# Attention features in (d, h) order, token-major q and k by DMA transposes, second layer norm normalised on ScalarE

## The chip, the cores and the metric

The kernel runs on one core of one Trainium2 chip. The metric is the device time of one execution in microseconds (us). Runs are compared by the median of several executions, and one further execution is profiled.

The engines of the core are named as in the profile: PE (TensorE, matrix multiply), DVE (VectorE), ACT (ScalarE), POOL (GpSimd) and SP (SyncE, which here only issues DMAs). Each works through its own instruction queue in order, and waits on semaphores for the others. DMAs are issued from SP, POOL and ACT.

## What is computed

One transformer block on 2048 tokens of 512 features in bfloat16, forward and backward. The kernel returns the output and the gradients of seven inputs.

```python
def A(x, wqkv, wo):                      # 32 heads of 16 features
    q, k, v = split(x @ wqkv)            # (2048, 1536) -> 3 x (32, 2048, 16)
    idx = pos[:, None] - 2 * arange(8)   # window of 8, dilation 2
    logits = einsum("hsd,hswd->hsw", q, k[:, idx]) / 4   # -1e9 where idx < 0
    o = einsum("hsw,hswd->hsd", softmax(logits), v[:, idx])
    return o.transpose(...).reshape(2048, 512) @ wo

def B(x, w1, b1, w2, b2):                # 512 -> 1792 -> 512
    return gelu(x @ w1 + b1) @ w2 + b2

h  = x + A(layernorm(x), wqkv, wo)
h2 = h + B(layernorm(h), w1, b1, w2, b2)
# outputs: h2 and the gradients of x, wqkv, wo, w1, b1, w2, b2 for a given grad_out
```

## The kernel before

**Three phases.** Tokens come in NC = 4 chunks of CH = 512. Phase 1 (lines 326 to 525) is the first layer norm and the attention, with the second layer norm at its end. Phase 2 (lines 570 to 643) is the feed-forward block, forward and backward; its first piece, `p2_h(0)`, is interleaved with the end of phase 1 (lines 712 to 717). Phase 3 (lines 882 to 1196) is the attention's backward pass and the weight gradients. The last two phases keep what they need of phase 1 in DRAM.

**Two layouts of q, k and v.** The projection `p1_proj` (line 341) makes q, k and v feature-major: a tile `qt`, `kt` or `vt` has 128 features on its partitions, 4 groups g of them, and 512 tokens along its rows. The features come in the order of the weight's columns, (h, d): head first, then the 16 features of a head. So one group of 128 partitions holds 8 whole heads.

The products with the window (`dots`, line 233) are made in this layout. DVE multiplies q with eight shifted views of k (line 236), and PE adds up the 16 features of each head with a 0/1 matrix `Emat[:, g]` (line 240), which puts the 8 heads of group g into 8 of 32 rows.

The weighted sums (`band`, line 257) need token-major rows instead. POOL gathers them with an indirect DMA (`gather_rows`, line 225) from DRAM tiles `v_d`, `k_d`, `q_d` and `go_d`, whose rows hold the features in the order (d, h). DVE multiplies them with the coefficients (line 266), and PE adds up with the 0/1 matrix `S32` (line 271). Phase 1 reads `v_d` only; `k_d`, `q_d` and `go_d` are read in phase 3 (line 1010).

**`to_tm_store` (line 208)** makes the token-major rows. For half a chunk, 8 PE transposes of 128x128 (line 214) go to a PSUM tile `ptm`; ACT copies it to `tmst` (line 217); SP stores it (line 219), with a copy of the border rows into the neighbour's tile (lines 221 and 223). The transposes multiply by a permutation `Pmat` and write with a stride, which turns (h, d) into (d, h). It runs for v in `p1_v`, for k and q in `p1_tm`, and for the gradient `got` in phases 2 and 3.

**Order of phase 1.** The program order is that of `p1_round(c)` (line 487): layer norm of chunk c+2, window products of c+1, output projection and second layer norm of c-1 (`p1_d`), q and k of c+2 (`p1_qk`), softmax of c+1, weighted sums of c in two halves (`p1_o`) around v of c+1 (`p1_v`), and last `p1_tm(c+1)`. The framework's scheduler then orders each engine's queue by its own estimates of when work is ready, so the order on an engine differs from that of the program. Tiles that share a tag share buffers, and the framework adds the waits.

**`layernorm` (line 169).** DVE makes the statistics of each 128-token tile (lines 173 and 174), POOL raises the variance to the power -1/2 (line 178), DVE makes `nm`, minus mean times that (line 180), and DVE normalises the four tiles (line 182). PE then transposes the result (`to_fm`, line 166) and ACT copies the transposes out (line 167). It runs for `xt` in `p1_ln` and for `h` in `p1_d`.

**Start.** `p1_ln(0)` loads the first rows of x and then the three parts of `wqkv` straight into the tile that the projection reads (line 333).

Of the kernel before, what the change touches and what calls it, by code (L numbers as in the profile page):

```python
# [10 lines left out]
P = 128  # L11
# [5 lines left out]
H = 32  # L17
# [19 lines left out]
def kernel(  # L37
# [70 lines left out]
    make_identity(nc, ident[:])  # L108
    Pmat = const.tile([P, P], BF16, name="Pmat")
    S32 = const.tile([P, 32], BF16, name="S32")  # L110
    Sum4 = const.tile([P, P], BF16, name="Sum4")
    nSum4 = const.tile([P, P], BF16, name="nSum4")
    Sm = const.tile([P, 4, P], BF16, name="Sm")
    ind8 = const.tile([P, 8], BF16, name="ind8")
    Emat = const.tile([P, 4, 32], BF16, name="Emat")
    mk = const.tile([16, 2, 4, 32], BF16, name="mk")
# [18 lines left out]
    v_d, k_d, q_d, go_d = ([dram.tile([RB, D], BF16, name=f"{n}_d{c}") for c in range(NC)] for n in ("v", "k", "q", "go"))  # L135
    vf_d = dram.tile([P, 4, SP], BF16, name="vf_d")
    ln1_d = dram.tile([S, D], BF16, name="ln1_d")
    ln2_d = dram.tile([S, D], BF16, name="ln2_d")
# [29 lines left out]

    def layernorm(wp, src, rstd_all, c, dst):
        mv = wp.tile([P, TPC, 2], F32, name="mv", tag="mv", bufs=2)  # L170
        for j in range(TPC):
            st = wp.tile([P, 6], F32, name="st6", tag="st6", bufs=2)
            V.bn_stats(out=st[:], in_=src[:, j, :])
            V.bn_aggr(out=mv[:, j, :], in_=st[:])
        rs = rstd_all[:, c * TPC:(c + 1) * TPC]
        ve = wp.tile([P, TPC], F32, name="ve", tag="ve", bufs=2)
        V.tensor_scalar(out=ve[:], in0=mv[:, :, 1], scalar1=EPS, scalar2=None, op0=ALU.add)
        G.tensor_tensor(out=rs, in0=ve[:], in1=mhalf[:], op=ALU.pow)
        nm = wp.tile([P, TPC], F32, name="nm", tag="nm", bufs=2)
        V.scalar_tensor_tensor(out=nm[:], in0=mv[:, :, 0], scalar=-1.0, in1=rs, op0=ALU.mult, op1=ALU.mult)  # L180
        for j in range(TPC):
            V.tensor_scalar(out=dst[:, j, :], in0=src[:, j, :], scalar1=rs[:, j:j + 1], scalar2=nm[:, j:j + 1],
                            op0=ALU.mult, op1=ALU.add)

# [22 lines left out]

    def to_tm_store(wp, fm, off, dst, c, back, nb=3, stage=None):
        for j2 in range(TPC // 2):
            pt = TT("ptm")  # L210
            for jj in range(2):
                j = 2 * j2 + jj
                for g in range(4):
                    T.transpose(_sub(pt[:], [[32, DH], [1, 8]], jj * 512 + 8 * g),  # L214
                                fm[:, g, off + j * P:off + (j + 1) * P], Pmat[:])
            st = stage() if stage else wp.tile([P, 2, 512], BF16, name="tmst", tag="tmst", bufs=nb)
            A.copy(out=st[:], in_=pt[:].rearrange("p (a n) -> p a n", a=2))  # L217
            r = j2 * 2 * P + (RPAD if back else 0)
            SY.dma_start(out=dst[c][r:r + 2 * P, :].rearrange("(a p) d -> p a d", p=P), in_=st[:])
            if back and j2 == 1 and c + 1 < NC:  # L220
                SY.dma_start(out=dst[c + 1][0:RPAD, :], in_=st[P - RPAD:P, 1, :])
            if not back and j2 == 0 and c > 0:
                SY.dma_start(out=dst[c - 1][CH:CH + RPAD, :], in_=st[0:RPAD, 0, :])

    def gather_rows(R, dst, c, sc, back):
# [7 lines left out]
    def dots(wp, ql, kw_, L, mask):  # L233
        for g in range(4):
            pr = wp.tile([P, W, 512], BF16, name="pr", tag="prod", bufs=2 + (wp is not late))
            V.tensor_tensor(out=pr[:], in0=ql[:, g, :].unsqueeze(1).to_broadcast([P, W, 512]),  # L236
                            in1=_sub(kw_[:, g, PAD:PAD + 512], [[-DIL, W], [1, 512]]), op=ALU.mult)
            for hf in range(2):
                for w4 in range(4):
                    T.matmul(L[hf][32 * w4:32 * w4 + 32, :], lhsT=Emat[:, g, :], rhs=pr[:, 2 * w4 + hf, :],  # L240
                             start=(g == 0), stop=(g == 3), skip_group_check=True)
        if mask:
            for hf in range(2):
                T.matmul(L[hf][:, 0:16], lhsT=mk[:, hf].rearrange("p a b -> p (a b)"), rhs=ident[0:16, 0:16],
                         start=False, stop=True, skip_group_check=True)
# [80 lines left out]
    def p1_ln(c):  # L326
# [3 lines left out]
        if c == 0:  # L330
            for i in range(3):
                o = (1, 0, 2)[i] * D
                SY.dma_start(out=wqkv[:, :, o:o + D], in_=A_wqkv[:, o:o + D].rearrange("(a p) j -> p a j", p=P))
        ln1 = early.tile([P, TPC, D], BF16, name="ln1", tag="ln1", bufs=2)
        layernorm(early, xt, rstd1, c, ln1)
        store_rows(ln1_d, c, ln1)
# [4 lines left out]
    def p1_proj(c, sel, dst, off, gs=range(4)):  # L341
        for g in gs:
# [4 lines left out]
            A.copy(out=dst[:, g, off:off + CH], in_=ps[:])  # L347

    def p1_qk(c):
        qt = early.tile([P, 4, CH], BF16, name="qt", tag="qt", bufs=2)  # L350
        kt = early.tile([P, 4, PAD + CH], BF16, name="kt", tag="kt", bufs=2)
        if c == 0:
            V.memset(kt[:, :, 0:PAD], 0.0)
            zz = early.tile([P, 4, PAD], BF16, name="zz", tag="zz")
            V.memset(zz[:], 0.0)
            G.dma_start(out=vf_d[:, :, 0:PAD], in_=zz[:])
        else:
            V.tensor_copy(out=kt[:, :, 0:PAD], in_=st_[c - 1]["kt"][:, :, CH:CH + PAD])
        for g in range(4):
            p1_proj(c, 1, kt, PAD, [g])  # L360
            p1_proj(c, 0, qt, 0, [g])
        st_[c].update(qt=qt, kt=kt)

    def p1_v(c):
        vt = early.tile([P, 4, PAD + CH], BF16, name="vt", tag="vt", bufs=1)
        p1_proj(c, 2, vt, PAD)
        to_tm_store(early, vt, PAD, v_d, c, True)
        G.dma_start(out=vf_d[:, :, PAD + c * CH:PAD + (c + 1) * CH], in_=vt[:, :, PAD:PAD + CH])

    def p1_tm(c):  # L370
        to_tm_store(early, st_[c]["kt"], PAD, k_d, c, True)
        to_tm_store(early, st_[c]["qt"], 0, q_d, c, False)

# [61 lines left out]
    def p1_d(c):  # L435
# [10 lines left out]
        ln2 = late.tile([P, TPC, D], BF16, name="ln2", tag="ln2", bufs=1)  # L446
        layernorm(late, ht, rstd2, c, ln2)
        store_rows(ln2_d, c, ln2)
# [5 lines left out]
    p1_ln(0)  # L454
    V.tensor_copy(out=_sub(Pmat[:], [[1, 8], [8, DH]]), in_=_sub(ident[:], [[DH, 8], [1, DH]]))
    for j in range(4):
# [4 lines left out]
    for j in range(4):  # L461
        V.tensor_copy(out=Sm[32 * j:32 * j + 32, j, :], in_=Sum4[32 * j:32 * j + 32, :])
    with nc.allow_low_precision(reason="exact 0/1 sums"):
        V.tensor_reduce(out=ind8[:], in_=ident[:].rearrange("p (a b) -> p a b", b=DH), axis=mybir.AxisListType.X, op=ALU.add)
    V.memset(Emat[:], 0.0)
    for g in range(4):
        V.tensor_copy(out=Emat[:, g, 8 * g:8 * g + 8], in_=ind8[:])
    G.memset(mk[:], 0.0)
# [15 lines left out]
    for a_, b_, t_ in w1:  # L484
        G.dma_start(out=t_[:], in_=B_w1[:, a_ * P:b_ * P].rearrange("(a p) f -> p a f", p=P))
    p1_tm(0)
    def p1_round(c):
        if c + 2 < NC:
            p1_ln(c + 2)
        if c == 0:  # L490
            for (d_t, r) in ((v_d[0], 0), (k_d[0], 0), (q_d[NC - 1], CH), (go_d[NC - 1], CH)):
                SY.dma_start(out=d_t[r:r + RPAD, :], in_=zrow[:])
            SY.dma_start(out=b1b[:], in_=B_b1.rearrange("(f p) -> f p", p=P))
            SY.dma_start(out=b2row[:], in_=B_b2.rearrange("(a n) -> a n", a=1))
# [18 lines left out]
        p1_o(c, 1)  # L513
        p1_tm(c + 1)
        if c == 1:
# [146 lines left out]
    def ga_sum(L, pr, g):  # L662
        for hf in range(2):
            for w4 in range(4):
                T.matmul(L[32 * w4:32 * w4 + 32, hf, :], lhsT=Emat[:, g, :], rhs=pr(2 * w4 + hf),
                         start=(g == 0), stop=(g == 3), skip_group_check=True)
# [9 lines left out]
    def p3_pre():  # L676
# [6 lines left out]
        SY.dma_start(out=vw[:], in_=vf_d[:, :, 0:PAD + CH])  # L683
        to_tm_store(ffp["B"], got, 0, go_d, 0, False, stage=lambda: ft("tst", "tmst0")[:, 0:8, :].rearrange("p (a b) f -> p a (b f)", a=2))
        yield
        L = [X("ps_ga0") for _ in range(2)]
        for g in range(4):
            pr = ft("xa", "pr0")
            ga_prod(pr[:].rearrange("p a b n -> p (a b) n"), got, vw, g)
            for hf in range(2):  # L690
                for w4 in range(4):
                    w = 2 * w4 + hf
                    T.matmul(L[hf][32 * w4:32 * w4 + 32, :], lhsT=Emat[:, g, :], rhs=pr[:, w // 4, w % 4, :],
                             start=(g == 0), stop=(g == 3), skip_group_check=True)
# [64 lines left out]
    for c in range(NC):  # L759
        if c == 2:  # L760
            load_wT("woT", A_wo)
            load_wT("wqT", A_wqkv[:, 0:D])
# [279 lines left out]
    def p3_go(c, at=(1, 2, 3, 4)):  # L1042
# [12 lines left out]
        def t():  # L1055
            to_tm_store(p3, got, 0, go_d, c, False, stage=lambda: pt3("tmst"))
        for n, cost, f in zip(at, (1.0, 1.8, 1.8, 1.0), (a, b(0), b(2), t)):
# [180 lines left out]
```

## Time and profile before

| | us |
|---|---|
| median of 3 runs | 669.7 (665.3 to 674.3) |
| profiled execution | 670.48 |
| its span, first to last instruction | 668.5 |
| PE busy | 610.2 (91%) |
| DVE busy | 513.8 (77%) |
| ACT busy | 367.0 (55%) |
| POOL busy | 154.5 (23%) |
| mean granted PE clock | 0.992 of full speed |

The span is shorter than the time by what lies around the program. Busy shares are averages over the three phases: phase 1 ends near 170 us with `p2_h(0)` beside it, phase 2 near 370 us, and phase 3 takes the rest. A line such as `L217 ACT COPY tmst<-ptm 128x1024 ... x24 | 23.6, 1021 | 4.8 <-PE ...` is one group of instructions: line of the kernel, engine, operation, output and input tile, shape, count, then busy us and mean ns of one, then the idle us of the engine just before them and what ended it. In a timeline, rows of several instructions give the time from the first's start to the last's end.

### The profile page before, as it was taken

The numbers are of one execution on the slowest core, as the hardware profiler recorded it, in microseconds if no ns is written. First come the engines' busy times: TensorE is split into PE (matmuls) and PEld (weight loads), VectorE is DVE, ScalarE is ACT, GpSimd is POOL, SyncE is SP. The second block draws the span as 40 slices with busy tenths as digits, with TensorE's granted clock in tenths as the row PEclk, the third lists the DMA queues.
The fourth block names the chain that finished last, engine by engine and source line by source line (L and its number), as shares of the span: only waits on it lengthen the run. The fifth ranks groups of instructions, "written<-read, shape, count | busy, mean of one in ns | idle before, by whom it ended". The sixth has DMA issues, their size and how long they took to land. (4 is left out here: it accounts for less than half of the span.)

```text
span 668.5 us, 10258 instructions
## 1 busy us (share of the span) xinstructions
PE 610.2 (91%) x3948; PEld 285.4 (43%) x3948; DVE 513.8 (77%) x758; ACT 367.0 (55%) x570; POOL 154.5 (23%) x183
## 2 busy tenths in 40 slices
PE   3888989788999899999999898999999999988997
PEld 1443434333443344444343433434456576433443
DVE  7989989969789769869839698887987898295400
ACT  2588877697783455645340362862494256463311
POOL 3341635432001111110100242220323134030100
PEclk9999999898999999999999999999999999999999
DMA  8583848735999999987987999884899689969141
GB/s 263 184 296 121 295 135 309 241 127 127 233 200 265 206 230 217 213 232 183 257 220 184 259 340 391 324 313 165 283 400 328 220 279 357 300 238 316 50 157 48
DMA packets 147806, 158.87 MB, mean 238 GB/s; under 512 B 94461, under 2 KB 132398, under 8 KB 141102
## 3 DMA queue, kind: packets, MB, share of 16 engines
q1 hardware_dynamic: 120078, 69.58, 40.8%
q0 software_dynamic: 15376, 77.63, 33.7%
q10 hardware_dynamic: 12304, 11.01, 5.2%
q8 instruction: 31, 0.51, 0.3%
q14 instruction: 17, 0.14, 0.1%
HBM read 87.63 MB, written 48.03 MB: 203 GB/s over the span
## 5 line engine op out<-in xcount | busy, mean ns | idle before, releaser
L1021 DVE TENSOR_TENSOR prb<-R,cf 128x2048 bf16<-128x2048 bf16 x96 | 110.9, 1220 | 7.4 <-DMA R<-k_d,rowi 3.2
L188 ACT ACTIVATE gyr<-ps_gl,rstd 128x512 bf16<-128x512 f32 x32 | 21.9, 687 | 77.9 <-PE ps_gl L1084 32.0
L583 PE MATMUL ps_h<-ln2T,w 128*128 128x512 bf16 x224 | 55.8, 379 | 0.8 <-ACT xa L585 0.4
L913 PE MATMUL ps_gw<-gwm,ln_r 128*128 128x256 bf16 x448 | 53.1, 273 | 2.6 <-DMA gwm<-ghT_d 1.7
L905 PE MATMUL ps_gw<-gout_r,gwm 128*128 128x512 bf16 x224 | 52.9, 380 | 2.7 <-DMA gwm<-gT_d 2.7
L628 PE MATMUL ps_gg<-goT,w2T 128*128 128x512 bf16 x224 | 54.6, 378 | 0.3 <-DVE gb1p L630 0.3
L615 PE MATMUL ps_f<-w,gt 128*128 128x512 bf16 x224 | 51.6, 379 | 3.0 <-DVE gt L591 3.0
L639 PE MATMUL ps_gl<-w1T,dt 128*128 128x512 bf16 x224 | 52.3, 379 | 1.6 <-ACT gyr L188 1.3
L659 DVE TENSOR_TENSOR pr<-got,vw 128x4096 bf16<-128x4096 bf16 x16 | 36.3, 2290 | 16.2 <-DMA gout_r<-in_grad_out_dram 11.4
L345 PE MATMUL ps_qkv<-ln1T,wqkv 128*128 128x512 bf16 x192 | 48.0, 393 | 0.7 <-ACT ln1T L167 0.6
L913 PEld LDWEIGHTS <-ln_r 128*128 128x128 bf16 x448 | 42.5, 98 | 14.3 <-issue 6.5
L584 ACT ACTIVATE xb<-ps_h,b1c 128x512 bf16<-128x512 f32 x56 | 38.6, 696 | 15.6 <-DVE xa L595 10.2
L630 DVE CUSTOM_DVE_ANT_0 dt<-ps_gg,dt 128x512 bf16<-128x512 f32 x56 | 37.7, 686 | 9.7 <-PE ps_gg L628 9.6
L933 PE MATMUL ps_gwq<-gqh,ln_r 128*128 128x512 bf16 x192 | 42.6, 379 | 1.2 <-ACT gwst L832 1.2
L585 ACT ACTIVATE xa<-ps_h,b1c 128x512 bf16<-128x512 f32 x56 | 38.7, 700 | 8.6 <-DVE dt L596 8.6
L568 POOL DMA_DIRECT2D gT_d<-tst x16 | 12.1, 757 | 124.3 <-DMA tst<-gt 122.2
L266 DVE TENSOR_TENSOR prb<-R,cf 128x2048 bf16<-128x2048 bf16 x32 | 37.6, 1210 | 2.5 <-DMA R<-v_d,rowi 1.5
L1031 ACT ACTIVATE gks<-ps_band 128x512 bf16<-128x512 f32 x32 | 19.0, 598 | 36.6 <-PE ps_band L1029 31.5
L236 DVE TENSOR_TENSOR pr<-qt,kt 128x4096 bf16<-128x4096 bf16 x16 | 36.1, 2285 | 2.1 <-PE ps_band L271 1.1
L590 ACT ACTIVATE xa<-xa 128x2048 bf16<-128x2048 bf16 (+1 forms) x16 | 27.1, 1700 | 14.3 <-DVE xa L589 14.2
L217 ACT COPY tmst<-ptm 128x1024 bf16<-128x1024 bf16 x32 | 31.3, 1020 | 6.2 <-PE ptm L214 3.3
L639 PEld LDWEIGHTS <-dt 128*128 128x128 bf16 x224 | 21.4, 98 | 30.2 <-issue 3.0
(186 smaller groups left out, 1134.3 us busy)
## 6 DMA issues: line engine op xcount, KB each, us to landing
gwm<-ghT_d SPq DMA_DIRECT2D x7, 1024.0 KB
gT_d<-tst POOLq DMA_DIRECT2D x12, 512.0 KB
ghT_d<-tst POOLq DMA_DIRECT2D x12, 512.0 KB
gwm<-gT_d SPq DMA_DIRECT2D x6, 1024.0 KB
out_dram<-gwst ACTq DMA_DIRECT2D x22, 256.0 KB
ln_d<-ln POOLq DMA_DIRECT2D x8, 512.0 KB
vw<-vf_d SPq DMA_DIRECT2D x4, 528.0 KB
xt<-in_A_x_dram SPq DMA_DIRECT2D x4, 512.0 KB
```

The costliest lines, as they stand in the source:

```text
L345: T.matmul(ps[:], lhsT=wqkv[:, dc, sel * D + g * P:sel * D + (g + 1) * P], rhs=st_[c]["ln1T"][:, dc, :], start=(dc == 0), stop=(dc == DC - 1))
L583: T.matmul(ps[:], lhsT=wcol(w1, dc, f), rhs=ln2T[c][:, dc, :], start=(dc == 0), stop=(dc == DC - 1))
L584: A.activation(out=xb[:, f - f0, :], in_=ps[:], func=ACT.Identity, bias=b1c[:, f:f + 1])
L585: A.activation(out=x2[:, f - f0, :], in_=ps[:], func=ACT.Square, bias=b1c[:, f:f + 1])
L615: T.matmul(ps[:], lhsT=gts[f // 4][:, f % 4, j * P:(j + 1) * P], rhs=wrow(w2, f), start=(f == 0), stop=False)
L628: T.matmul(ps[:], lhsT=wcol(w2T, dc, f), rhs=goT[:, dc, :], start=(dc == 0), stop=(dc == DC - 1))
L630: V.tensor_tensor_reduce(out=dsl, in0=ps[:], in1=dsl, scale=1.0, scalar=0.0, op0=ALU.mult, op1=ALU.add, accum_out=gb1p[:, f, c:c + 1])
L639: T.matmul(ps[:], lhsT=dts[f // 4][:, f % 4, j * P:(j + 1) * P], rhs=wrow(w1T, f), start=(f == 0), stop=(f == FT - 1))
L905: yield from mm_pair("ps_gw2", lambda ps, o, u, i, t, k: T.matmul(ps[:], lhsT=g_[:, o, i * HN + t, :], rhs=gout_r[i][:, t, :], **k), MM, w ...
L913: yield from mm_pair("ps_gw1", lambda ps, o, u, i, t, k: T.matmul(ps[:, 256 * u:256 * u + 256].rearrange("p (a f) -> p a f", a=2), lhsT=ln ...
L933: yield from mm_pair("ps_gwq", lambda ps, o, u, i, t, k: T.matmul(ps[:], lhsT=ln1_r[i][:, t, (2 * d2 + o) * P:(2 * d2 + o + 1) * P], rhs=h ...
L1021: V.tensor_tensor(out=pr[:, 4 * hf:4 * hf + 4].rearrange("p j (d h) -> p j d h", h=H), in0=R[:, o:o + 4, :].rearrange("p j (d h) -> p j d ...
```

## The change

Three edits go together.

1. The columns of `wqkv` are brought into (d, h) order when they are loaded. The three parts are loaded as they are into spare tiles, and six strided copies (four on ACT for k and q, two on POOL for v) write them into `wqkv` permuted. Then `qt`, `kt` and `vt` have features in (d, h) order: a group of 128 partitions holds 4 features of all 32 heads. `Emat` gives way to `S32` in all window sums, and `Pmat` to the identity in the transposes. The rows of `wo` are copied within DRAM into the same order (`woP_d`), and the transposed `woT` of the backward pass is loaded from there.
2. The token-major q and k of phase 1 are made by DMA transposes issued on SP from `kt` and `qt`, four for each tensor and chunk, into a tile of the whole chunk, which one DMA stores. `p1_tm` is called at the end of `p1_qk`. v and `got` keep PE transposes and ACT copies, now with contiguous output.
3. The second layer norm's four normalisations of a chunk are done by ACT instead of DVE. The first layer norm stays on DVE.

```diff
-    Pmat = const.tile([P, P], BF16, name="Pmat")
-    ind8 = const.tile([P, 8], BF16, name="ind8")
-    Emat = const.tile([P, 4, 32], BF16, name="Emat")
+    woP_d = dram.tile([D, D], BF16, name="woP_d")
...
-    def layernorm(wp, src, rstd_all, c, dst):
+    def layernorm(wp, src, rstd_all, c, dst, aj=()):
...
         for j in range(TPC):
-            V.tensor_scalar(out=dst[:, j, :], in0=src[:, j, :], scalar1=rs[:, j:j + 1], scalar2=nm[:, j:j + 1],
-                            op0=ALU.mult, op1=ALU.add)
+            if j in aj:
+                A.activation(out=dst[:, j, :], in_=src[:, j, :], func=ACT.Identity, scale=rs[:, j:j + 1], bias=nm[:, j:j + 1])
+            else:
+                V.tensor_scalar(out=dst[:, j, :], in0=src[:, j, :], scalar1=rs[:, j:j + 1], scalar2=nm[:, j:j + 1],
+                                op0=ALU.mult, op1=ALU.add)
...
+    def to_tm_pe(fm, dst, c, stage):
+        for j2 in range(TPC // 2):
+            pt = TT("ptm")
+            for jj in range(2):
+                for g in range(4):
+                    T.transpose(pt[:, jj * 512 + g * P:jj * 512 + (g + 1) * P],
+                                fm[:, g, (2 * j2 + jj) * P:(2 * j2 + jj + 1) * P], ident[:])
+            st = stage()
+            A.copy(out=st[:], in_=pt[:].rearrange("p (a n) -> p a n", a=2))
+            r = j2 * 2 * P
+            SY.dma_start(out=dst[c][r:r + 2 * P, :].rearrange("(a p) d -> p a d", p=P), in_=st[:])
...
+    def to_tm_store(wp, fm, off, dst, c, back, nb=2, stage=None):
+        st = stage() if stage else wp.tile([P, TPC, D], BF16, name="tmst", tag="tmst", bufs=nb)
+        for g in range(4):
+            SY.dma_start_transpose(out=st[:, :, g * P:(g + 1) * P], in_=fm[:, g, off:off + CH])
+        r = RPAD if back else 0
+        SY.dma_start(out=dst[c][r:r + CH, :].rearrange("(a p) d -> p a d", p=P), in_=st[:])
+        if back and c + 1 < NC:
+            SY.dma_start(out=dst[c + 1][0:RPAD, :], in_=st[P - RPAD:P, TPC - 1, :])
+        if not back and c > 0:
+            SY.dma_start(out=dst[c - 1][CH:CH + RPAD, :], in_=st[0:RPAD, 0, :])
...
-                    T.matmul(L[hf][32 * w4:32 * w4 + 32, :], lhsT=Emat[:, g, :], rhs=pr[:, 2 * w4 + hf, :],
+                    T.matmul(L[hf][32 * w4:32 * w4 + 32, :], lhsT=S32[:], rhs=pr[:, 2 * w4 + hf, :],
...
         if c == 0:
-            for i in range(3):
-                o = (1, 0, 2)[i] * D
-                SY.dma_start(out=wqkv[:, :, o:o + D], in_=A_wqkv[:, o:o + D].rearrange("(a p) j -> p a j", p=P))
+            wraw = wff.tile([P, 2, DC, D], BF16, name="wraw", tag="w10", bufs=1)
+            wrav = wff.tile([P, DC, D], BF16, name="wrav", tag="w18", bufs=1)
+            raws = [wraw[:, 1], wraw[:, 0], wrav[:]]
+            for i in (1, 0, 2):
+                SY.dma_start(out=raws[i], in_=A_wqkv[:, i * D:(i + 1) * D].rearrange("(a p) j -> p a j", p=P))
+
+            def by_dh(i, put, lo, hi):
+                put(out=wqkv[:, :, i * D + lo * H:i * D + hi * H].rearrange("p a (d h) -> p a d h", h=H),
+                    in_=raws[i].rearrange("p a (h d) -> p a d h", d=DH)[:, :, lo:hi, :])
+            by_dh(1, A.copy, 0, 8)
+            by_dh(1, A.copy, 8, 16)
+            by_dh(0, A.copy, 0, 8)
+            by_dh(0, A.copy, 8, 16)
+            by_dh(2, G.tensor_copy, 0, 8)
+            by_dh(2, G.tensor_copy, 8, 16)
...
         st_[c].update(qt=qt, kt=kt)
+        p1_tm(c)
...
         p1_proj(c, 2, vt, PAD)
-        to_tm_store(early, vt, PAD, v_d, c, True)
+        for j2 in range(TPC // 2):
+            pt = TT("ptm")
...
+            st = early.tile([P, 2, D], BF16, name="vtm", tag="vtm", bufs=2)
+            A.copy(out=st[:], in_=pt[:].rearrange("p (a n) -> p a n", a=2))
+            r = j2 * 2 * P + RPAD
+            SY.dma_start(out=v_d[c][r:r + 2 * P, :].rearrange("(a p) d -> p a d", p=P), in_=st[:])
...
-        layernorm(late, ht, rstd2, c, ln2)
+        layernorm(late, ht, rstd2, c, ln2, (0,1,2,3))
...
+            G.dma_start(out=woP_d[:].rearrange("(d h) n -> d h n", h=H), in_=A_wo.rearrange("(h d) n -> d h n", d=DH))
...
-        p1_tm(c + 1)
...
-            load_wT("woT", A_wo)
+            load_wT("woT", woP_d[:])
```

## The prediction

> **What bounds the kernel now.** I read the engines' busy time by stretches first, because the change touches the first quarter of the span and the shares of the whole page mix it with the rest. Columns: stretch, its length, busy time and instructions of PE, PE weight loads, DVE, ACT, POOL, then PE clock, DMA share, GB/s.
>
> ```profile
> 12.00:46.00 34.00, 30.16 (x219) 14.29 (x222) 30.86 (x62) 24.08 (x38) 14.51 (x14) 1.00 0.67 219
> 46.00:64.00 18.00, 17.33 (x136) 7.11 (x129) 17.68 (x16) 12.66 (x22) 2.91 (x5) 1.00 0.43 160
> 64.00:96.00 32.00, 29.34 (x258) 13.88 (x250) 27.44 (x36) 25.50 (x40) 14.15 (x14) 1.00 0.65 219
> 96.00:125.00 29.00, 24.52 (x220) 11.35 (x213) 28.03 (x36) 22.01 (x34) 15.04 (x15) 1.00 0.80 262
> 125.00:147.00 22.00, 18.77 (x145) 9.04 (x142) 17.73 (x26) 18.12 (x27) 8.98 (x14) 0.92 0.62 208
> 147.00:170.00 23.00, 16.48 (x72) 6.64 (x71) 19.51 (x30) 18.71 (x28) 5.15 (x6) 0.85 0.59 118
> 170.00:270.00 100.00, 95.51 (x425) 40.12 (x424) 81.71 (x145) 57.04 (x88) 10.57 (x14) 1.00 1.07 226
> 270.00:370.00 100.00, 98.50 (x485) 42.17 (x485) 77.75 (x148) 43.02 (x76) 10.40 (x14) 1.00 0.89 216
> ```
>
> From 170 us on PE is full (95.5 and 98.5 of 100). The change takes nothing there but the output stride of 64 transposes, so I book 0 there. All that can be won lies before 170, where no one engine is full everywhere: DVE from 46 to 64 and from 96 to 125, PE and DVE together elsewhere, ACT in parts of the end. The next rows, groups of instructions up to 200 us, give the durations of what goes (count, then busy us and mean ns).
>
> ```profile
> L217 ACT COPY tmst<-ptm 128x1024 bf16<-128x1024 bf16 x24 | 23.6, 1021 | 4.8 <-PE ptm L214 2.1 <-ACT vt L347 1.6 <-ACT ost L429 1.0
> L182 DVE TENSOR_SCALAR ln<-h,rstd,nm 128x512 bf16<-128x512 bf16 x16 | 5.5, 407 | 0.0
> L214 PE MATMUL ptm<-Pmat,qt 128*128 128x128 bf16 x64 | 5.2, 231 | 0.8 <-ACT tmst L217 0.8
> L214 PE MATMUL ptm<-Pmat,kt 128*128 128x128 bf16 x64 | 5.1, 219 | 0.4 <-ACT tmst L217 0.4
> L584 ACT ACTIVATE xb<-ps_h,b1c 128x512 bf16<-128x512 f32 x26 | 18.0, 700 | 0.6 <-DVE gb1p L630 0.4 <-PE ps_h L583 0.2
> ```
>
> Last the timeline, at the places where the new DMA transposes can hurt (start, us, instruction): a DMA transpose of 128x2048 and its reader; the v store of chunk 1, the gather that reads it and the DVE product that reads the gather; and the one long PE gap.
>
> ```profile
> 150.75 1.95 SPq L567 DMA_TRANSPOSE tst<-gt  x1
> 155.64 0.78 POOL L568 DMA_DIRECT2D gT_d<-tst  x1 [7.81 <-DMA tst<-gt]
> ...
> 64.42 1.28 SPq L219 DMA_DIRECT2D v_d<-tmst  x2
> 69.79 2.57 POOL L228 DMA_INDIRECT R<-v_d,rowi  x1 [0.60 <-DVE pr L236]
> 80.08 1.18 DVE L266 TENSOR_TENSOR prb<-R,cf 128x2048 bf16<-128x2048 bf16 x1
> 151.55 1.86 PE L442 MATMUL ps_wo<-wo,oT 128*128 128x512 bf16 x4 [4.00 <-ACT xa L585]
> ```
>
> The reader sees: 0.5 MB transposed from SBUF to SBUF is usable 4.9 us after its issue; the gather waits for a DVE product, not for the store; and PE stops for 4 us behind ACT.
>
> **What the Trainium skill says.** "DMA: Bandwidth & Descriptors", section Anatomy of one DMA: a semaphore wait is served by the issuing sequencer before dispatch, so a DMA whose input is late holds all behind it on its queue. The trace agrees: SP spends 104.7 us at L219 waiting for ACT's tmst. The same page, section Latency and other measured facts, gives 261 GB/s for one kernel's DMA transposes; here woT, w2T, goT and w1T, 4.72 MB, take 163.4 to 192.3 us in the queue, 163 GB/s, and I use that. "TensorE: Matmul & The Clock Gate", Part 1, What's actually happening: after an idle window of some 3.4 us PE drops to half clock. Agreed: after the 4.0 us gap the granted clock is 0.59 from 151.6 to 158. "ScalarE: Activation LUTs", section What ACT_TABLE_LOAD costs: an ACTIVATE takes 186 ns + 0.833 ns per element, 93 ns more for each per-partition operand; neighbours overlap by 93 ns. For L584 that is 706 ns against 700 measured.
>
> **The change part by part.**
>
> *Token-major q and k by DMA.* Gone are 128 PE transposes (L214, kt and qt) and 16 ACT copies (L217). On the timeline 16 such transposes take 1.15 us and two copies 1.93, so PE loses 128/16 x 1.15 = 9.2 us and ACT 8 x 1.93 = 15.4, in each chunk 2.3 and 3.9. Added are 32 DMA transposes of 128x512, eight per chunk. At 163 GB/s one takes 0.8 us of all DMA engines: 26 us in 150, on shares of 0.43 to 0.80, so there is room. SP's issue is 1.95/4 = 0.5 us each, and SP is mostly idle. Latency from issue to use is not in the trace for this size. Upper bound: the 4.9 us of the size four times larger. Lower: its share of issue and data, about 1.3. I take 2.5, the eight overlapping.
>
> What they delay: in the built order of SP's queue the v stores of chunk 1 stand behind all eight transposes of chunk 2 and its k and q stores, which wait for the transposes to land; those of chunk 2 stand behind chunk 3's. The last qt of chunk 2 is written at 57.0 us: 57.0 + 2.5 + four stores at 0.4 = 61.1, and the v store was ready at 64.4. For chunk 3: 89.3 + 4.1 = 93.4 against 96.0. So the transposes are hidden by 3.3 and 2.6 us. If that cover goes, 3.0 us more lie between store and gather (69.79 - 64.42 is 5.4; the first chunk's gather came 2.35 us after its last store), and about 3 between gather and product (a gather lands within 8.1 us, 120.4 to 128.5). Queued behind a late gather on POOL is the power of chunk 0's second layer norm.
>
> *Permuted weights.* Four ACT copies of 128x1024 with a strided read: L284, which reads PSUM with a stride, takes 1.03 us, so 3.9 together. ACT idles until 11.4 us at the start. wk is in by 7.2 to 8.2 us (SP's slot waits end at 8.2 and 9.7 for the next two), so the copies end at 11.1 to 12.1. If SBUF reads with this stride cost double, 15. I take +0.5, bounds 0 and +3.6. Two POOL copies: "GPSIMD Engine Reference", section 3.1, has 1.8 to 2.6 cycles an element, an estimated 1.5 to 2.2 us each; POOL then reaches its next power at 16.7 to 18.0 instead of 17.27, under DVE's products from 18.5 to 22.9: 0, bounds 0 and +1. The row copy of wo in DRAM is one POOL issue of 0.8 us and read 100 us later: 0. Selectors: DVE loses Pmat, ind8, Emat, zz, 1.4 us; S32 has Emat's shape, so the 128x32 matmuls cost the same. v and go keep PE transposes and copies.
>
> *Second layer norm on ACT.* DVE loses 4 x 1.38 = 5.5 us (four take 1.38 on the timeline). ACT gains 16 activations with two per-partition operands, which no row shows: L584's pace, one per 0.57 us, below, the page's 799 ns above; I take 799 - 93 = 0.7, so 11.2 us, 2.8 a chunk (2.3 to 3.2). New wait: ACT now stands for nm, which DVE makes after POOL's power (DVE waits 0.9 to 1.2 us there). Behind it on ACT are casts of q and k and the ln2T copies, and PE waits for their PSUM.
>
> *By stretch.* 0 to 12: +0.5. 12 to 46: PE -2.3, ACT -3.9, DVE -1.4, of 34 with DVE and PE about 90% full: -1.5. 46 to 64: DVE full, nothing of it goes: 0. 64 to 96: PE -2.3, ACT -3.9 + 2.8, DVE -1.4: -1.5. 96 to 125: DVE full, -1.4. 125 to 170: ACT loses 3.9 and gains 5.6 (two chunks) where it was full from 158 to 165; DVE -2.8, PE -2.3: 0, bounds -2 and +4. Sum -3.9. The profiled execution took 670.48 (span 668.5 and 2.0 around it): 666.6. The median shown, 669.7, lies 0.8 lower: 665.8. Forecast 666.
>
> **The rivals.** *PE is the bound after all.* PE's busy time tops most stretches, and then all 9.2 us count: 661. Against it: 46 to 64 and 96 to 125.
>
> *The new ACT wait eats it.* Four waits of about 1.5 us for nm, 1.8 us more ACT work at the end, and a longer PE gap with 2 to 3 us at half clock: 6 to 7 back, 673. For it: ACT fills 4.59 of 4.60 us in the gap. Against it: DVE and POOL reach nm earlier with DVE relieved.
>
> *The DMA transposes run one at a time and hold SP.* This ends slower. At t us each, v of chunk 1 goes out at 48.6 (first kt) + 8t + 1.6. With the 6 us of slack behind 64.4 it decides from t = 2.5. At 4 us it is 11.8 late, and for chunk 3 (79.3 + 33.6 against 96.0 + 6) 10.9: +22.7 - 3.9, 689. At 4.9 both grow by 7: 704. For it: SP serves waits in order, and transposes issued in a row stretched to 5.8 us of issue. Against it: those ran at DMA shares above 1, here about 0.6 to 0.9.
>
> That the change doesn't happen is excluded: the built order has 256 PE rows fewer and 32 transposes on SP.
>
> **How the numbers follow.** Forecast (662 to 669) 0.50, PE bound (656 to 662) 0.12, ACT wait or nothing gained (669 to 680) 0.24, SP held (680 to 704) 0.14. Range 659 to 681: outside it are most of the last case and a few hundredths below. A measurement of this kernel tells no change from about 2%, 656.3 to 683.1: faster 0.04, same 0.83, slower 0.13.
>
> **What would show it.** Right: PE's first full stretch, now from 170, starts some 4 us earlier; v stores within a us of their old place relative to vt; the gather waits for DVE, not v_d. Wrong: POOL waiting for v_d or DVE for R (SP held); ACT waiting for nm by over a us each time with PE on ACT casts (ACT wait); the first matmul of L345 after 14 us (strided weight copies); DMA transposes of 128x512 landing after 2.5 us.

## The result, and the profile after

The changed kernel takes 691.0 us (median of 4, 688.4 to 696.1) against 669.1 us (median of 4, 665.3 to 674.3) for the kernel before on the same chip: a ratio of 1.033, with a 95% interval of 1.023 to 1.043. It is slower, by about 22 us. The profiled execution took 688.4 us with a span of 686.5, at a mean TensorE clock of 0.968 (before: 668.5 and 0.992). All ratios leave out executions more than 1.5% above the fastest of their kernel, which matters in one run, named below.

The stretches of the prediction up to 170 us, then two later ones, now of the changed kernel (length; busy time and instructions of PE, PE weight loads, DVE, ACT, POOL; PE clock; DMA share; GB/s):

```profile
12.00:46.00 34.00, 27.03 (x180) 11.89 (x180) 31.54 (x55) 22.02 (x34) 11.18 (x12) 1.00 0.97 233
46.00:64.00 18.00, 15.22 (x94) 5.22 (x95) 15.63 (x15) 10.91 (x19) 5.85 (x5) 0.91 0.88 259
64.00:96.00 32.00, 20.93 (x165) 9.50 (x165) 19.51 (x29) 18.52 (x29) 10.73 (x15) 0.89 0.99 221
96.00:125.00 29.00, 23.45 (x175) 10.18 (x178) 23.39 (x24) 17.37 (x28) 6.80 (x11) 0.88 0.82 202
125.00:147.00 22.00, 15.78 (x115) 6.87 (x114) 16.08 (x21) 15.20 (x23) 8.33 (x12) 0.77 0.78 271
147.00:170.00 23.00, 15.61 (x98) 6.90 (x100) 16.83 (x23) 18.66 (x26) 8.03 (x13) 0.88 0.38 121
170.00:190.00 20.00, 14.08 (x67) 5.94 (x67) 17.18 (x26) 18.54 (x27) 4.79 (x5) 0.93 0.75 164
190.00:290.00 100.00, 99.03 (x428) 42.03 (x436) 82.78 (x148) 57.26 (x92) 10.52 (x14) 0.98 0.98 224
```

PE is full only from about 190 us, not from 170: the whole loss lies ahead of that. The worst stretch is 64 to 96, with PE at 20.9 of 32 (29.3 before) and DVE at 19.5 (27.4). There the DMA share rose from 0.65 to 0.99 while the GB/s stayed at 221 (219 before): the engines are busy, but move no more. The clock falls behind PE's gaps: with no matmul at all from 86 to 90 us, it is 0.50 from 90 to 98.

Groups of instructions up to 200 us (count, then busy us and mean ns, then idle time before and its releasers):

```profile
L275 DVE TENSOR_TENSOR prb<-R,cf 128x2048 bf16<-128x2048 bf16 x32 | 37.6, 1212 | 18.7 <-DMA R<-v_d,rowi 18.7
L181 ACT ACTIVATE ln<-h,nm,rstd 128x512 bf16<-128x512 bf16 x16 | 11.7, 807 | 8.9 <-DVE nm L178 5.8 <-issue 3.1
L237 POOL DMA_INDIRECT R<-v_d,rowi x8 | 8.7, 1092 | 40.3 <-DMA v_d<-vtm 22.6 <-DVE prb L275 10.7 <-DVE mv L172 6.0
L347 ACT COPY wqkv<-wraw 128x1024 bf16<-128x1024 bf16 x4 | 7.8, 2031 | 3.9 <-DMA wraw<-in_A_wqkv_dram 3.9
L347 POOL COPY wqkv<-wrav 128x1024 bf16<-128x1024 bf16 x2 | 4.0, 2034 | 0.1
```

Both signs that I had named for a held SP are there: POOL's gather waits 22.6 us for v_d and DVE's product 18.7 us for R. So is the sign for the strided weight copies, as the projection's first matmul starts at 14.74 us, after 14. The wait for v_d falls on two gathers, in chunk 0 (10.56 us) and in chunk 1 (12.08), and round 1 is the worst place. First SP's queue, then what follows from it on POOL, DVE and ACT (start, us, instruction, idle time before it and its releaser):

```profile
42.39 1.08 SPq L400 DMA_DIRECT2D v_d<-vtm  x2
...
64.97 2.58 SPq L226 DMA_TRANSPOSE tmst<-kt  x2
67.65 3.46 SPq L226 DMA_TRANSPOSE tmst<-qt  x2
71.15 2.37 SPq L226 DMA_TRANSPOSE tmst<-kt  x1
73.57 1.35 SPq L226 DMA_TRANSPOSE tmst<-qt  x1
...
80.56 1.80 SPq L400 DMA_DIRECT2D v_d<-vtm  x2
```

```profile
46.62 1.10 POOL L237 DMA_INDIRECT R<-v_d,rowi  x1 [10.56 <-DMA v_d<-vtm]
...
85.96 1.05 POOL L237 DMA_INDIRECT R<-v_d,rowi  x1 [12.08 <-DMA v_d<-vtm]
88.32 1.05 POOL L176 TENSOR_TENSOR rstd<-ve,mhalf 128x4 f32<-128x4 f32 x1
89.40 0.16 DVE L178 SCALAR_TENSOR_TENSOR nm<-mv,rstd 128x4 f32<-128x4 f32 x1 [5.76 <-POOL rstd L176]
89.66 2.93 ACT L181 ACTIVATE ln<-h,nm,rstd 128x512 bf16<-128x512 bf16 x4 [5.42 <-DVE nm L178]
96.29 4.63 DVE L275 TENSOR_TENSOR prb<-R,cf 128x2048 bf16<-128x2048 bf16 x4 [5.73 <-DMA R<-v_d,rowi]
```

v of chunk 0 lies ready in vtm at 36.9 us and its store is issued at 42.39, behind the transposes of its own chunk. v of chunk 1 lies ready at 69.1 us, but its store is issued at 80.56, behind eight transposes of chunk 2 and four stores. The gather follows, and the power behind the gather; nm waits for the power, and ACT waits 5.4 us for nm, with chunk 3's casts of q and k behind it.

### The profile page after: what moved, and what is told of

The parts are those of the page before. It is cut to its first block, busy times and chain, and to the rows that moved or that the text cites. A ratio compares the mean times of both kernels' runs of the same rounds, so it can differ in the third digit from the quotient of the medians.

```text
span 686.5 us, 9972 instructions
## 1 busy us (share of the span) xinstructions
PE 605.8 (88%) x3761; PEld 281.1 (41%) x3820; DVE 511.7 (75%) x734; ACT 372.0 (54%) x574; POOL 148.7 (22%) x186
## 3 DMA queue, kind: packets, MB, share of 16 engines
q1 hardware_dynamic: 137358, 73.78, 43.6%
## 5 line engine op out<-in xcount | busy, mean ns | idle before, releaser
L639 PE MATMUL ps_f<-w,gt 128*128 128x512 bf16 x220 | 53.0, 387 | 2.7 <-ACT ln2T L165 2.0
L663 PE MATMUL ps_gl<-w1T,dt 128*128 128x512 bf16 x218 | 50.9, 379 | 0.8 <-ACT gyr L189 0.4
L275 DVE TENSOR_TENSOR prb<-R,cf 128x2048 bf16<-128x2048 bf16 x32 | 37.6, 1212 | 18.7 <-DMA R<-v_d,rowi 18.7
L957 PE MATMUL ps_gwq<-gqh,ln_r 128*128 128x512 bf16 x188 | 42.2, 379 | 0.8 <-ACT gwst L856 0.6
L592 POOL DMA_DIRECT2D gT_d<-tst x16 | 12.1, 755 | 123.7 <-DMA tst<-gt 123.3
L293 ACT COPY gqkvT<-ptu 128x1024 bf16<-128x1024 bf16 x24 | 24.3, 1011 | 18.6 <-PE ptu L292 18.6
L607 PEld LDWEIGHTS <-w 128*128 128x128 bf16 x224 | 22.2, 101 | 29.4 <-issue 6.8
```

Of the source, the lines that this page charges most:

```text
L607: T.matmul(ps[:], lhsT=wcol(w1, dc, f), rhs=ln2T[c][:, dc, :], start=(dc == 0), stop=(dc == DC - 1))
L639: T.matmul(ps[:], lhsT=gts[f // 4][:, f % 4, j * P:(j + 1) * P], rhs=wrow(w2, f), start=(f == 0), stop=False)
L663: T.matmul(ps[:], lhsT=dts[f // 4][:, f % 4, j * P:(j + 1) * P], rhs=wrow(w1T, f), start=(f == 0), stop=(f == FT - 1))
L957: yield from mm_pair("ps_gwq", lambda ps, o, u, i, t, k: T.matmul(ps[:], lhsT=ln1_r[i][:, t, (2 * d2 + o) * P:(2 * d2 + o + 1) * P], rhs=h ...
```

## The experiments

Three theories stood after this reading. T1: v's stores stand behind the DMA transposes on SP's queue. T2: the transposes fill the DMA engines, so that stores and gathers take longer wherever they are issued. T3: the second layer norm on ACT, with its chain through POOL and DVE, costs the time. All ratios are against the kernel before, with 95% intervals.

**v's stores on ACT's queue.**

```
-            SY.dma_start(out=v_d[c][r:r + 2 * P, :]...
+            A.dma_start(out=v_d[c][r:r + 2 * P, :]...
```

> The changed kernel with one thing altered: v's three stores per chunk are issued by ScalarE, not by SyncE, so that they no longer stand behind the eight DMA transposes of q and k on SyncE's queue. T1 (SyncE's queue: transposes at about 1.45 us each, 11.6 us for eight, stand before v's stores, the gathers wait 2 to 23 us for v_d): the waits of POOL's gather for v_d fall under 3 us each and the kernel comes to 672 to 678 us. T2 (the DMA engines themselves: share 0.9 to 1.0 until 125 us, so each gather takes 9 to 17 us wherever its rows come from): the store is earlier but VectorE waits for R as long as before; 684 to 691 us. T3 (the chain through POOL's rstd, VectorE's nm and ScalarE's normalisation is what costs): 686 to 691 us, with POOL's gather no longer waiting.

687.4 us, 1.032 [1.026, 1.039]: nothing is won. But POOL waited only 14.6 us for v_d and DVE only 3.0 for R, and a new wait came up on ACT's timeline:

```profile
65.33 1.93 ACT L398 COPY vtm<-ptm 128x1024 bf16<-128x1024 bf16 x2 [0.70 <-PE ptm L395]
78.61 1.63 ACTq L400 DMA_DIRECT2D v_d<-vtm  x2
82.04 0.59 ACT L446 CAST rb<-ps_r 128x512 bf16<-128x512 f32 x1 [14.78 <-DMA tmst<-kt]
```

The store's data is ready at 67.3 and it is issued at 78.6; the idle time ends with a transpose of chunk 2, of which v's store uses nothing. The built program explains the wait: each DMA of SP and ACT has one of eight completion counters, handed out in turn, and waits until the DMA that had it last has landed. So the run didn't take v out from behind the transposes. It moved the wait to ACT, where it stops more. It tells T1 from T2 less than I had meant.

**The transposes at their old place in the code.** The call p1_tm goes back behind p1_o(c, 1).

> The changed kernel with the call that transposes and stores token-major q and k put back to where the kernel before has it, after v and after the second half of the attention output; the DMA transposes stay. T1 (position in SyncE's queue): as v's stores on ScalarE or a little better, 670 to 677 us, v_d of each chunk written within 5 us of its copy. T2 (DMA engines): the same bytes in the same 150 us, 682 to 691 us; VectorE still waits for R. T3 (second layer norm's chain): 686 to 691 us.

695.3 us, 1.039 [1.031, 1.047]. In the trace SP's queue keeps the order of the changed kernel nevertheless: transposes of chunk 2 from 65.9, v's store at 82.9. The place in the code doesn't set the place on the queue here, so the run says nothing on T1.

**q and k by TensorE.** The DMA transposes go, weights and ACT's layer norm stay.

```
-            SY.dma_start_transpose(out=st[:, :, g * P:(g + 1) * P], in_=fm[:, g, off:off + CH])
+            T.transpose(pt[:, jj * 512 + g * P:...], fm[:, g, off + j * P:off + (j + 1) * P], ident[:])
...
+            A.copy(out=st[:], in_=pt[:].rearrange("p (a n) -> p a n", a=2))
```

> The changed kernel with q and k made token-major by TensorE transposes and ScalarE copies of PSUM, at the place where the kernel before does it; the weights in (d, h) order and ScalarE's second layer norm stay. T1 and T2 alike (the DMA transposes are the cause, by queue or by engines): 668 to 674 us, of which the start's later first projection (14.7 against 12.5 us) keeps about 2. T3 (ScalarE's layer norm with its waits is the cause): 680 us or more.

674.7 us, 1.010 [1.007, 1.013]. Two thirds of the loss go with the DMA transposes. Some 1% is left, more than the later start was expected to keep.

**ACT's second layer norm alone**, on the kernel before.

> The kernel before with the second layer norm's four normalisations on ScalarE and nothing else changed. T1 and T2: 667 to 671 us, no change that can be measured; ScalarE waits for nm under 1 us a chunk. T3: 674 us or more, ScalarE waiting for nm some 5 us in one round.

1.010 [1.006, 1.014], where T1 and T2 said no change. So T3 holds in part: about 7 us, without any DMA transpose. Its mechanism, a wait for nm of some 5 us, is not there: in the profiled execution the longest such wait is 1.0 us.

**The second layer norm back on DVE**, in the changed kernel: `layernorm(late, ht, rstd2, c, ln2, ())`.

> The changed kernel with the second layer norm's normalisation back on VectorE; weights and DMA transposes stay. Additive (the layer norm costs the same 1.0% as it does on the kernel before, because ScalarE sets the pace of the start of the feed-forward, where its eight normalisations of the last two chunks stand in the same queue as the casts and GELUs): 682 to 685 us. T3 (in the changed kernel the normalisations also stand behind a gather that waits for v, so that they cost more there): under 680 us. If the transposes' delay hides the layer norm: 688 us or more.

686.8 us, 1.032 [1.024, 1.039]. Beside the transposes ACT's layer norm costs no more than the runs can tell (1.033 with it). The two costs don't add up. That ACT has time again where v's lateness holds all engines is a reading that no run tests.

**The weights alone**: q and k by TensorE and the layer norm on DVE.

> The weights in (d, h) order alone: q and k by TensorE transposes at the old place, the second layer norm on VectorE. If the sum is additive (674.7 us with ScalarE's layer norm, which is worth 7 to 8): 666 to 669 us, no change, the first projection still at about 14.7 us. If the later start costs what it shows: 670 us or more.

667.5 us, 1.001 [0.999, 1.003]: no change, though the first projection starts at 14.71 us instead of 12.48.

**v's stores on POOL's queue**, whose counters are its own.

> The changed kernel with v's stores issued by GpSimd, whose DMAs go through the software queue and neither stand on SyncE's queue nor wait for the completion counters that SyncE's and ScalarE's DMAs share (with the stores on ScalarE the issue waited 14.8 us for a transpose of the next chunk). If the place of v's stores behind the transposes is the cause, by queue or by counters: 674 to 680 us, POOL's gather waiting for v_d under 3 us each time. If the DMA engines' load is the cause: 685 to 692 us, with the store's own landing or the gather's over 10 us.

679.2 us, 1.016 [1.009, 1.023]: half of the loss is gone, and with it most of POOL's wait for v_d (6.5 us in all, 3.4 the longest). This is T1 for about half of the loss, with the shared counters as part of the queue. The other half is not split further. DVE still waits 16.7 us for R, and a gather took up to 19.5 us to land, as T2 has it; but POOL, which now issues the stores, also waits 11.9 us for ACT's vtm before them, and its own later work waits behind.

**The same with the second layer norm on DVE.**

> The changed kernel with two things altered: v's stores issued by GpSimd and the second layer norm back on VectorE. What stays over the kernel before is the DMA transposes without the place they gave v's stores. Additive (679 with GpSimd's stores, of which 7 to 8 for ScalarE's layer norm): 670 to 674 us, VectorE still waiting some 10 us for R, whose rows come later while the DMA engines are full. If the load on the engines costs nothing: 665 to 669 us.

1.007 [1.002, 1.012], some 4.5 us, but that ratio keeps only 5 of 20 executions. All 20 lie between 667.9 and 698.3 us with a median of 683.1, 1.022 of the kernel before (median 668.6), whose 39 executions stayed between 665.2 and 677.8. So what the transposes cost, once v's stores don't stand behind them, is 4.5 us in the best executions and about 14 in the median one. Against 1.032 with the stores on SP, moving them is worth between 1.0% and 2.5%, and this run doesn't settle how the loss divides between v's place on the queue and the rest. The profiled execution (670.9 us) is one of the five: DVE still waits 10.2 us for R. What delays the others was not traced.

**Transposes added to the kernel before**, their results unused, and two runs with plain copies in their place.

```
+        for fm_, of_ in ((kt, PAD), (qt, 0)):
+            for g in range(4):
+                dm = early.tile([P, TPC, P], BF16, name="dm", tag="dm", bufs=5)
+                SY.dma_start_transpose(out=dm[:], in_=fm_[:, g, of_:of_ + CH])
```

> The kernel before, with eight DMA transposes of 128x512 per chunk added behind the projections of q and k; what they write is read by nobody, and q and k go to DRAM by TensorE as before. If the transposes hurt because they are there (SyncE's queue, its completion counters, the DMA engines), and not because their own result is late: 680 to 688 us, v_d late again and POOL's gather waiting for it over 8 us. If only the result's lateness matters: 667 to 670 us.

> The same with eight plain DMA copies in place of the transposes: the same source, the same bytes in the same 256-byte pieces to a place of the same shape, and the same order on SyncE's queue. If it is being a transpose that costs (1.2 us and more on SyncE's queue each, and the engines' slow handling): 667 to 671 us. If any DMA of this many pieces does it: as with the transposes.

> The run with plain copies again, whose 1 KB rows were contiguous on both sides and went out in 144 packets a copy where a transpose takes 544: now each row is written in four pieces of 256 bytes to places 4 bytes apart, so that a copy has about as many pieces as a transpose. If the number of pieces is what fills the DMA engines: 676 to 684 us, the DMA share over 1.0 between 46 and 64 us and the gather waiting for v. If it is the transposing itself: 667 to 672 us, the hardware queue's time within some 10 us of the run with contiguous copies.

Transposes: 679.7 us, 1.014 [1.006, 1.022]. Plain copies: 668.6 us, 1.000 [0.997, 1.003]; their expectation was wrong on the pieces, since rows contiguous on both sides went out in 144 packets a copy (4,608 more on the hardware queue for 32 copies), where 32 transposes add 17,408, 544 each. With four pieces a row (528 packets a copy): 668.8 us, 1.003 [1.000, 1.006]. So neither the bytes nor the number of pieces explains more than some 2 us, and the rest is the transposing. Here are the hardware queue's packets, MB and share of 16 engines' span, of the kernel before, with transposes, and with copies in 256-byte pieces:

```profile
q1 hardware_dynamic: 120078, 69.58, 40.8%
```

```profile
q1 hardware_dynamic: 137486, 73.78, 46.1%
```

```profile
q1 hardware_dynamic: 136974, 73.78, 43.9%
```

Over the spans (668.5, 678.2, 664.3) that is 272.7, 312.6 and 291.6 us: 39.9 us more for the transposes, 18.9 for the copies. On SP's timeline, with the same order of instructions, transposes first, then copies in pieces:

```profile
61.79 6.75 SPq L365 DMA_TRANSPOSE dm<-kt  x4
68.59 5.33 SPq L365 DMA_TRANSPOSE dm<-qt  x4
73.97 1.08 SPq L219 DMA_DIRECT2D v_d<-tmst  x2
```

```profile
54.21 2.70 SPq L365 DMA_DIRECT2D dm<-kt  x4
56.96 2.76 SPq L365 DMA_DIRECT2D dm<-qt  x4
64.47 1.28 SPq L219 DMA_DIRECT2D v_d<-tmst  x2
```

The chunk's transposes hold SP for 12.1 us, the copies for 5.5; with the copies v's store keeps its old time (64.42 before), with the transposes it is 9.6 us late. The sign that I had named, a wait of POOL for v_d of over 8 us, didn't come: it waited 3.8 us, DVE 5.7 us for R, and ACT 4.8 us for a tmst buffer that v's store still held. And 1.4% is less than half of what the transposes cost in the changed kernel (1.032 less 1.001). There k's and q's stores, ahead of v's on SP, also wait for the transposes to land; no run separates that part.

**Two transposes of 128x2048 in place of eight.**

> The same with two DMA transposes of 128x2048 per chunk in place of eight of 128x512: the same bytes, a quarter of the instructions. If the number of instructions is what costs (issue time on SyncE's queue, completion counters): 668 to 673 us. If the bytes through the DMA engines cost: within 4 us of the run with eight.

682.1 us, 1.022 [1.013, 1.031]: a quarter of the instructions saves nothing that shows. One of them held SP for 16.7 us, and POOL waited up to 10.6 us for v_d:

```profile
41.18 16.69 SPq L364 DMA_TRANSPOSE dm<-kt  x1
...
79.49 1.01 POOL L228 DMA_INDIRECT R<-v_d,rowi  x1 [10.56 <-DMA v_d<-tmst]
```

Both gathers of chunk 0 were issued at 37.9 and 40.4 and their products ran from 52.4 to 63.0; the hold ends in that time. The long holds of the other runs, too, lie where gathers are in flight (6.4 us from 51.1 in the changed kernel). It isn't the transposes' alone: in the run with copies in pieces one copy of the same chunk held SP for 4.5 us, and four together took 10.4 us from 42.2. That gathers and the DMAs on SP hold one another up is one reading; no run separates it from other waits of the queue (for a counter, or for a buffer, of which there is one here and five above). It stays open.

**The second layer norm on ACT in two chunks only**, with the weights in order and q and k on TensorE: `(0,1,2,3) if c < 2 else ()`, and the reverse.

> Weights in (d, h) order, q and k by TensorE as before, and ScalarE normalises the second layer norm of chunks 0 and 1 alone; VectorE does chunks 2 and 3. If the 7 us that ScalarE's layer norm costs come from chunks 2 and 3, whose eight activations stand among ScalarE's casts of the first feed-forward: 664 to 669 us, as the weights alone or a little faster, since VectorE is relieved of 2.8 us while it is full. If each chunk costs its share, or the wait for nm is what costs: 670 to 672 us.

> The same with ScalarE normalising chunks 2 and 3 alone. If the cost lies in the feed-forward's start: 673 to 676 us, all of it. If each chunk costs its share: 670 to 672 us.

670.5 us, 1.004 [1.001, 1.008], and 672.6 us, 1.006 [1.003, 1.009]. Both pairs cost, 2 to 3 us and about 4 us. That all of it comes from chunks 2 and 3 is not met; equal shares of some 3.5 us lie within both intervals. The wait for nm is small with TensorE's transposes (1.0 us in all with four chunks on ACT). The delay can be followed, in the weights alone and then with all four chunks on ACT:

```profile
153.82 1.11 ACT L480 CAST h<-ps_wo 128x512 bf16<-128x512 f32 x2
167.28 1.48 DVE L183 TENSOR_SCALAR ln<-h,rstd,nm 128x512 bf16<-128x512 bf16 x4
169.32 1.93 ACT L165 COPY ln2T<-pt 128x1024 bf16<-128x1024 bf16 x2 [0.60 <-PE pt L164]
170.69 3.40 PE L646 MATMUL ps_f<-w,gt 128*128 128x512 bf16 x15
```

```profile
139.37 2.94 ACT L181 ACTIVATE ln<-h,nm,rstd 128x512 bf16<-128x512 bf16 x4
157.01 1.11 ACT L480 CAST h<-ps_wo 128x512 bf16<-128x512 f32 x2
168.92 2.93 ACT L181 ACTIVATE ln<-h,nm,rstd 128x512 bf16<-128x512 bf16 x4 [0.37 <-DVE nm L178]
173.56 1.91 ACT L165 COPY ln2T<-pt 128x1024 bf16<-128x1024 bf16 x2
174.60 3.15 PE L646 MATMUL ps_f<-w,gt 128*128 128x512 bf16 x7 [1.97 <-ACT ln2T L165]
```

Chunk 2's four activations come at 139.4, among ACT's work on the first feed-forward; chunk 3's output is cast 3.2 us later, its own activations take 2.9 us where DVE's take 1.5, and PE's second feed-forward product starts 3.9 us later. It also starts slowly, as the stretch from 170 to 190 us shows in the same two runs (columns as above):

```profile
170.00:190.00 20.00, 19.72 (x88) 8.09 (x87) 14.57 (x19) 14.38 (x21) 0.00 (x0) 1.00 1.18 232
```

```profile
170.00:190.00 20.00, 16.77 (x74) 6.97 (x73) 14.62 (x19) 16.30 (x22) 1.56 (x2) 0.83 1.13 227
```

With the activations on ACT, from 175 to 180 us the granted clock is 0.51, with 13 matmuls where the weights alone have 23 at 1.00. All four runs with second layer norms on ACT and q and k on TensorE show it in their profiled execution, with 0.50 to 0.64 in the lowest 5 us between 170 and 180, the run with chunks 0 and 1 alone too (0.50 from 170 to 175). The kernel before and the weights alone stay at 1.00 there. So part of the cost is a longer gap of PE, followed by a lower clock. Where chunks 0 and 1 start to lose was not followed.

No version beats the kernel before; the weights alone equal it.

## Why the prediction was wrong

The forecast of 666 us failed at the step "SP's issue is 1.95/4 = 0.5 us each" (measured: 1.2 us at least, 1.6 on average in chunk 2), with what hung on it, "the transposes are hidden by 3.3 and 2.6 us". What happened is the third rival, the transposes that hold SP (689 us, chance 0.14; measured 691.0). That its number is so near is luck: it supposed 4 us a transpose on a queue that is free at 48.6 us, and neither was so.

*Token-major q and k by DMA: booked as a gain, measured +3.1%, 20 us (1.032 less 1.001).* The sum had three terms.
- SP's issue. I scaled one row of 128x2048 by its bytes. A 128x512 transpose holds SP for 1.2 us at least, with medians of 1.44 (k) and 1.48 (q), and up to 6.4. Chunk 2's eight took 64.97 to 78.1, not 4 us.
- The engines. "26 us" was right in the changed kernel: 43.6% of 686.5 less 40.8% of 668.5 is 26.6 us; added to the kernel before, the same transposes took 39.9. "So there is room" was not. I set an average over 150 us against a load in bursts, and the share came to 0.97, 0.88 and 0.99 in the first three stretches. What this load costs by itself is open: with v's stores elsewhere between 4.5 and about 14 us stay, as the run on POOL's queue without ACT's layer norm showed.
- The cover. It is gone in every chunk. The sum left out chunk 0, whose v goes out at 42.39 against 34.13, and POOL waits 10.6 us there. For chunk 1 v_d goes out at 80.56 against 64.42 (16.1 late), at 117.08 against 96.04 for chunk 2. The rival's point of decision, 2.5 us a transpose, was set too high. It counted from 48.6 us, the first kt, but chunk 1's transposes and stores kept SP until 63.9, so chunk 2's began at 64.97. Even at 1.6 us each they ended after v was due. I had priced each chunk's transposes on an empty queue. The eight shared counters, in the build before me, were not in the sum at all.

The argument against the rival, that stretched issues had run at DMA shares above 1 and "here about 0.6 to 0.9", fits the shares of before (0.43 to 0.80) with the transposes' 26 us spread evenly over 150; they came in bursts.

*Second layer norm on ACT: booked at 0 from 125 to 170 and inside a gain before, measured +0.9% to +1.0%, 6 to 7 us, where q and k stay on TensorE.* These runs keep the copies at L217 that the sum takes from ACT, so they don't measure the term as it was booked. In the changed kernel itself the layer norm costs no more than the runs can tell (1.033 against 1.032), and its part in the miss is not shown. The durations were right: 0.80 us each and four in 2.93, where I took 0.7 and 2.8. What is doubtful in "0, bounds -2 and +4" is that I set the 3.9 us that ACT was to lose at L217 against the 5.6 us that it gains. They lie at different places: the last copies of L217 end at 132.5 us on the timeline of before, and the activations stand at 139 and 169, ahead of the casts of h and the copy of ln2T. The second rival (673) had the size and part of the place: its longer PE gap with some us at half clock is there. Its four waits for nm are not; the longest is 1.0 us without the transposes, and 5.4 us only behind a late gather, where I had said the power would stand. Two or three us come with chunks 0 and 1, where I booked a gain.

*Permuted weights: booked +0.5 (0 to +3.6), measured 0.* The doubling for a strided SBUF read, my bad case, is what came (2.03 us against 1.03), and PE starts 2.2 us later. That it costs nothing at the end shows in the run of the weights alone; what takes it up was not traced.

*The range.* 681 as its upper end left out the right rival on purpose. What the profile gave for a chance above 0.14: the v store stands behind the transposes in the built order, and a single scaled row had to carry the number that decides.

## What to carry to other kernels

Price a DMA that is moved onto a queue by its hold on that queue, per instruction, with everything that is queued ahead of it, and then ask which store behind it somebody waits for. A DMA transpose is not a copy of the same bytes: here eight transposes in each chunk made the kernel 9 to 11 us slower, and as many copies in as many pieces about 2. Before relieving one engine at the cost of another, ask whether the other has slack in the same few microseconds: here the layer norm left DVE for ACT, and came out just ahead of the casts that the next stage waits for.

## What the runs showed of the hardware

- A DMA transpose of 128x512 bf16 held its issuing queue for 1.2 us at least and up to 10.1 us (transposes added), one of 128x2048 for 1.9 us at least and up to 16.7. A plain copy of the same 128x512 held it for 0.46 us at least in 1 KB rows, and for 0.59 us at least and up to 4.5 in 256-byte pieces.
- 32 transposes of 128x512 took 27 to 40 us of all 16 DMA engines, plain copies of the same data 8 (42.0% of 668.9 less 272.7) and, in 256-byte pieces, 19.
- ACT's copy of 128x1024 bf16 out of SBUF with a 32-byte stride takes 2.03 us, and POOL's takes the same; ACT's copy of as much out of PSUM with a 64-byte stride takes 1.03.
- In the changed kernel PE had no matmul from 86 to 90 us and was granted 0.50 of its clock from 90 to 98.
